# Attention scores of two heads of one half of the array per step, and products with v eight in a row

## Chip, cores and metric

One core of one Trainium2 chip. The metric is device time in microseconds (us) for one execution of the whole kernel; beside it stands one profiled execution whose trace is read here.

## What is computed

A transformer layer with attention and a feed-forward part side by side on the same normalised input: x is 2048 x 512, 32 heads of width 16, hidden width 1792.

```python
def _A_ref(x, wqkv, wo):
    qkv = (x @ wqkv).reshape(B, S, 3, H, Dh).transpose(2, 0, 3, 1, 4)
    q, k, v = qkv[0], qkv[1], qkv[2]
    scores = jnp.einsum("bhqd,bhkd->bhqk", q, k) * (Dh ** -0.5)
    p = softmax(scores, axis=-1)
    o = jnp.einsum("bhqk,bhkd->bhqd", p, v)
    return o.transpose(0, 2, 1, 3).reshape(B, S, D) @ wo

def _B_ref(x, w1, b1, w2, b2):
    return gelu(x @ w1 + b1) @ w2 + b2

xn = layernorm(A_x)
out = A_x + _A_ref(xn, A_wqkv, A_wo) + _B_ref(xn, B_w1, B_b1, B_w2, B_b2)
```

## The kernel before

The heads are worked in 8 groups of 4 (`NG`), the queries in 4 blocks of 512 (`NQB`); one head group and one query block is a `t`, and its 16 steps of 128 keys (or 128 queries for the maxima) are its units `u`, 512 units in all (`NU`). In each unit every one of the four heads gets two score products:

- **S** (`s_half`): scores with queries on the partitions, into a bank of the accumulator memory, of which VectorE takes the row maximum (`reduce_max` into `mt`, line 250). Three banks take turns.
- **T** (`e_half`): 20 units later (`LEAD`), when the maxima have gone through DRAM into the operand `qst`, the transposed scores with the maximum already subtracted; ScalarE writes exp of them into a tile `pe` (line 297). Three banks take turns.

**V** (`v_half`) multiplies the `pe` tiles in fp32 with v. Its sums stay in one bank for a whole `t`, the four heads in four quarters of 32 partitions. **D** is everything dense: the projections of q and k, the hidden layer (`hidden`, with a VectorE copy `hh` at line 978 and a chain on GpSimd), the product with `w2`, and at the end the output projection with `wo_s`. D comes in groups (`Group`), each summed in one bank and cut into 12 products (42 for `w2`) for each half of the array.

All four kinds are cut into products of 64 rows of operand and 32 output partitions (`tiled`), so the array works as two row halves, called side 0 and side 1, of four column quarters each. Heads 0 and 2 lie on side 0, heads 1 and 3 on side 1. V and D use both sides in turn, and both sides add into the same bank, so a side may begin only when the other has ended; a semaphore (`turns`, in `product`, `leave`, `enter`) orders that.

`unit` writes the order of the instructions by hand. A unit is two halves. Each half gives out the scores S side 0, T side 1, S side 1, T side 0, and then V for four heads on one side beside D on the other. The sides of V and D change in each half. D gives `pace` products to its side in each half: (4, 4) for `FAST`, (3, 4) for `MEAN`, (3, 3) for `SLOW`. A D group that ends hands its bank back at the end of the half.

`tick` runs once for each unit: it issues what was put off with `later` (transfers above all) and lets GpSimd have 2500 ns of queued work. All transfers go through the queue of SyncE.

Before the steady part stand about 140 us of normalisation, projection of the first heads and measuring of weights; behind it the last output projections.

Of the kernel before, what the change touches and what calls it, by code (L numbers as in the profile page):

```python
# [8 lines left out]
F32 = mybir.dt.float32  # L9
# [22 lines left out]
FAST, MEAN, SLOW = (4, 4), (3, 4), (3, 3)  # L32
MEASURE = (3, 0, 1, 2)
HALF = 1300
# [13 lines left out]
def layer_kernel(ctx: ExitStack, tc: tile.TileContext, x, wqkv, wo, w1, b1, w2, b2, out):  # L48
# [17 lines left out]
    w2_d = dram.tile([P, 2, NF, D], F16, name="w2_d")  # L66
    acc_d = dram.tile([S, D], F32, name="acc_d")
# [26 lines left out]
    wo_s = const.tile([P, 2, NC, D], F16, name="wo_s")  # L94
# [53 lines left out]
    def split_pool(hi, lo, src, inv):  # L148
        nc.scalar.activation(hi, src, AF.Copy, scale=inv)
        given("act", 1000)  # L150
        nc.gpsimd.tensor_scalar(src, src, inv, 0.0, op0=ALU.mult, op1=ALU.add)
        nc.gpsimd.tensor_tensor(lo, src, hi, op=ALU.subtract)
# [4 lines left out]
    backlog = {"act": 0, "dve": 0}  # L157

    def given(engine, ns):
        backlog[engine] += ns  # L160

    turns = tc.alloc_semaphore("turns")
    counted, left, newest, goal = [0], [], {}, [None]

    def product(user, *args, **kw):

        p = nc.tensor.matmul(*args, **kw)  # L169
        if user is None:  # L170
            return
        if goal[0] is not None:
            p._wait_ge(turns, counted[0])
            tc.declare_fence(p.ins, group=goal[0])
            goal[0] = None
        newest[user] = p

    def leave(user, goes_on):

        p = newest.pop(user, None)  # L180
        if p is not None and goes_on:
            p.then_inc(turns, 1)
            tc.no_tile_sem_insts.add(p.ins.name)
            counted[0] += 1
            left.append(p)

    def enter():

        if left:
            goal[0] = f"turn{counted[0]}"  # L190
            for p in left:
                tc.add_to_no_dep_group(goal[0], p.ins)
            left.clear()

    def tiled(user, dst, lhs, rhs, start, stop):

        for j in range(0, P, 32):
            product(user, dst[j:j + 32], lhs[:, j:j + 32], rhs, start=start, stop=stop)


    mt_of, ptiles, pv_of = {}, {}, {}
# [36 lines left out]
    def s_half(u, n):  # L238

        t, i = divmod(u, 16)  # L240
        g, qb = divmod(t, NQB)
        qt, kb = divmod(i, 4) if t else (i % 4, i // 4)
        if t not in mt_of:
            mt_of[t] = work.tile([P, 4, 4, 4], F32, name="mt", bufs=2)
        ks, qs = kst[g % 2], qst[g % 2]
        p, a = divmod(n, 2)
        r = slice(64 * a, 64 * a + 62)
        s = banks("S")
        tiled(None, s, qs[p][qb][r, qt * P:(qt + 1) * P], ks[p][kb][r, :], True, True)
        nc.vector.reduce_max(mt_of[t][:, n, qt, kb:kb + 1], s, axis=AX.X)  # L250
        given("dve", 600)

    def s_end(u):

        t, i = divmod(u, 16)
        if i < 15:
            return
        g, qb = divmod(t, NQB)
        qs = qst[g % 2]
        mneg = mnegs[t % 2]  # L260
        nc.vector.tensor_reduce(mneg[:, :16], mt_of[t].rearrange("p h t k -> p (h t) k"), axis=AX.X, op=ALU.max, negate=True)
        given("dve", 220)

        def store():

            pt = banks("S")
            for a in range(2):
                nc.tensor.matmul(pt[32 * a:32 * a + 32, :64], mneg[64 * a:64 * a + 64, :],
                                 ident[64 * a:64 * a + 64, 64 * a:64 * a + 64], start=True, stop=True)
            msb = work.tile([64, 64], F32, name="msb", bufs=2)  # L270
            nc.vector.tensor_scalar_mul(msb, pt[:64, :64], 1.0 / MROW)  # L271
            given("dve", 220)
# [12 lines left out]

    def e_half(u, n):
# [7 lines left out]
        tiled(None, st, kst[g % 2][p][kt // 4][r, k0:k0 + P], qst[g % 2][p][qb][r, :], True, True)  # L294
        pe = work.tile([P, QB], F32, name="pe", bufs=12)
        ptiles[u, n] = pe
        nc.scalar.activation(pe, st, AF.Exp, scale=sexp[:, g // 2:g // 2 + 1])  # L297
        given("act", 580)

    def v_half(u, a):  # L300

        t, kt = divmod(u, 16)
        g, qb = divmod(t, NQB)
        if kt == 0 and a == 0:
            pv_of[t] = hold("V", "S")
        pv = pv_of[t][0]
        r = slice(64 * a, 64 * a + 64)
        for h in (2, 3, 0, 1):
            c = (4 * g + h) * VW
            product("V", pv[32 * h:32 * h + 32, :], vv[r, kt, c:c + 32], ptiles[u, h][r],  # L310
                    start=(kt == 0 and a == 0), stop=(kt == 15 and a == 1))

    def v_end(u):

        t, kt = divmod(u, 16)
        g, qb = divmod(t, NQB)
        for h in range(4):
            del ptiles[u, h]
        if kt < 15:
            return  # L320
# [3 lines left out]
        given("act", 600)  # L324
# [12 lines left out]
        def inverse():  # L337
            nc.vector.reciprocal(dn, dn)
            given("dve", 330)
            later(1, lambda: nc.sync.dma_start(den_d[t, 1].rearrange("h (c q) -> (h c) q", q=32), dn))  # L340
# [63 lines left out]
    class Group:  # L404
# [15 lines left out]
        def product(self, side):  # L420
# [11 lines left out]
            tiled("D", self.bank, lhs[r], rhs[r], start, self.last and self.over())  # L432
# [43 lines left out]
    def project(m, w, sb, wh, bank, early=False):  # L476
# [6 lines left out]
        def finish(pj):  # L483
# [5 lines left out]
            given("act", 600)  # L489
# [62 lines left out]
    def ended():  # L552

        if cur[0] is not None and cur[0].over():
            done, cur[0] = cur[0], None
            done.end()
# [10 lines left out]
    def dense(gen, side):  # L567

        f = group(gen)
        for _ in range(0 if f is None else f.pace[pos[0] % 2]):  # L570
            if not f.usable(side):
                return
            f.product(side)

# [9 lines left out]
    def unit(gen):  # L584


        u = pos[0]
        e = u - LEAD
        if u == LEAD and cur[0] is not None:
            burst(gen, cur[0].left())  # L590
        pos[0] += 1
        for a in range(2):
            for b in range(2 * a, 2 * a + 2):
                if u < NU:
                    s_half(u, b)
                if 0 <= e < NU:
                    e_half(e, b ^ 1)
            if e >= 0:
                enter()

                w, r = (e - 2, 1) if a == 0 else (e - 1, 0)
                live = 0 <= w < NU
                new = r == 0 and w % 16 == 0
                if live and not new:
                    v_half(w, r)
                dense(gen, 1 - r)
                if live and new:
                    v_half(w, r)

                for user, goes_on in (("V", live and not (r == 1 and w % 16 == 15)),  # L610
                                      ("D", cur[0] is not None and not cur[0].over())):
                    leave(user, goes_on)
                for k in backlog:
                    backlog[k] = max(0, backlog[k] - HALF)
                if live and r == 1:
                    v_end(w)
                ended()
        if u < NU:
            s_end(u)
        if u < LEAD:  # L620
            burst(gen, LFILL[u - 16])
# [10 lines left out]
    with ExitStack() as st1:  # L632
# [16 lines left out]
        def absmax(dst, v):  # L649
            nc.vector.tensor_reduce(dst, v, axis=AX.XY if len(v.shape) == 3 else AX.X, op=ALU.max,  # L650
                                    apply_absolute_value=True)
            given("dve", 600)
# [229 lines left out]
        def prepare():  # L882
# [20 lines left out]
            for n in range(16):  # L903
# [5 lines left out]
                def then(wh=None, n=n):  # L909
# [8 lines left out]
                if n >= 14:  # L918
                    i = 2 * (n - 14)
                    split_steps(wo_s[:, 0, i:i + 2, :], wo_s[:, 1, i:i + 2, :], v, inv[:, 9:10], then)  # L920
                    continue
                wh = ph.tile([P, 2, 4, W] if n < 7 else [P, 2, 2, D], F16, name="wsp", bufs=2)
                k = n if n < 7 else 8
# [13 lines left out]
    def mlp():  # L937
# [5 lines left out]
        def gelu(hh, g, b, f):  # L943
            t1 = m2.tile([P, QB], F32, name="t1", bufs=2)

            def tanh():
                nc.scalar.activation(t1, t1, AF.Tanh, scale=GELU_C * GELU_A)
                given("act", 600)
# [14 lines left out]
        for b in range(NQB):  # L963
            xb = xbs[b]
            g = m2.tile([P, 2, NF, QB], F16, name="g", bufs=1)
            for f in range(NF):
# [8 lines left out]
                def hidden(hp, g=g, b=b, f=f):  # L975
# [3 lines left out]
                    given("dve", 700)  # L979
# [3 lines left out]
                             for c in range(NC) for i, j in PAIRS], dbank, hidden, pace=FAST if f % 2 else SLOW)  # L983
            for q in range(4):
# [7 lines left out]
                def store(yp, xa=xa, t=t):  # L992
                    yt = m2.tile([P, D], F32, name="yt", bufs=2)
                    nc.scalar.activation(yt, yp, AF.Copy, scale=gs[:, 2:3])  # L994
                    given("act", 600)
# [62 lines left out]
    with ExitStack() as st3:  # L1058
        p3 = pool(st3, "ph3")
        wo_l = p3.tile([64, 2, D], F16, name="wo_l")  # L1060
        nc.sync.dma_start(wo_l, wo_s[64:128, :, NC - 1, :])
# [67 lines left out]
```

## Time and profile before

| what | value |
|---|---|
| median of 3 runs | 1570.55 us (1565.78 to 1573.75) |
| the profiled execution | 1564.4 us, span 1562.6 us |
| granted TensorE clock | 0.992 of full speed |
| exps (line 297) / row maxima (line 250) | 2048 each, four of each in a unit |
| products of V / S / T, as instructions | 8192 each |

A step's time is read by counting exps in a stretch of the trace: four of them are one unit. TensorE, VectorE and ScalarE are each busy for most of the span, so a share of busy time says little; what counts in each stage is which of them the others wait for.

### The profile page before, as it was taken

How to read it: one execution, taken by the hardware profiler on the slowest of the kernel's cores; microseconds unless marked ns; L12 is line 12 of the kernel's file. 1: busy time of each engine (PE TensorE's matmuls, PEld its weight loads, DVE VectorE, ACT ScalarE, POOL GpSimd, SP SyncE). 2: the span in 40 equal slices, each digit the busy share in tenths (PEclk: the TensorE clock that was granted, in tenths of full speed). 3: DMA queues.
4: the chain of work that ended last, by engine and by line, in shares of the span. 5: the costliest groups of instructions: out<-in, count | busy, mean ns of one | idle time of the engine just before them, and what ended most of it. 6: DMA issues, size and time to landing. Idle time of an engine off the chain costs nothing.

```text
span 1562.6 us, 85974 instructions
## 1 busy us (share of the span) xinstructions
PE 1509.6 (97%) x38915; PEld 813.5 (52%) x38915; DVE 1419.0 (91%) x2388; ACT 1369.2 (88%) x2254; POOL 668.9 (43%) x742
## 2 busy tenths in 40 slices
PE   8997998989999999999999999999999999999998
PEld 4433554545555555555555555555555555554543
DVE  8886987989999999999999999999999999999911
ACT  4314997989999999999999999999999999999993
POOL 3113587737773111777411167751127773111000
PEclk9998999999999999999999999999999999999999
DMA  6467466351121111121111111221112100003123
GB/s 205 129 205 257 130 172 211 114 167 47 47 67 50 38 34 36 58 57 44 55 44 50 34 45 43 64 63 37 40 41 66 42 21 28 29 21 125 55 91 103
DMA packets 120248, 123.71 MB, mean 79 GB/s; under 512 B 38988, under 2 KB 90572, under 8 KB 119880
## 3 DMA queue, kind: packets, MB, share of 16 engines
q1 hardware_dynamic: 119880, 118.21, 25.0%
q8 instruction: 304, 4.98, 1.3%
q14 instruction: 64, 0.52, 0.1%
HBM read 80.61 MB, written 37.34 MB: 75 GB/s over the span
## 4 chain that ended last, share of the span: by engine, by line
PE 70%; DVE 21%; DMA 4%; issue 2%; POOL 1%; SPq 1%; ACT 1%; DVEq 0%; POOLq 0%
PE pV L169 21%; DVE mt L250 16%; PE pD L169 16%; PE pS L169 15%; PE pT L169 14%; DVE hh L978 2%; PE pD L428 1%; DMA wch<-in_B_w_dram 1%; PE pT L428 1%; DVE amx L650 1%; DMA dn<-den_d 1%; PE pT L521 1%; DMA m_d<-mhl 0%; PE pS L428 0%; DMA out_dram<-ac 0%
## 5 line engine op out<-in xcount | busy, mean ns | idle before, releaser
L297 ACT ACTIVATE pe<-pT,sexp 128x512 f32<-128x512 f32 x2048 | 1267.6, 688 | 72.8 <-PE pT L169 26.9
L250 DVE TENSOR_REDUCE mt<-pS 128x1 f32<-128x512 f32 x2048 | 1289.1, 683 | 34.4 <-PE pS L169 15.6
L169 PE MATMUL pV<-pe,vv 64*32 64x512 f32 x8192 | 1079.0, 597 | 1.4 <-PE pS L169 0.7
L169 PE MATMUL pT<-qst,kst 64*32 64x512 f16 x8192 | 706.9, 379 | 3.9 <-DMA qst<-m_d 1.4
L169 PE MATMUL pS<-kst,qst 62*32 62x512 f16 x8192 | 636.1, 379 | 35.6 <-DVE mt L250 32.1
L169 PEld LDWEIGHTS <-qst 62*32 62x32 f16 x8192 | 280.2, 92 | 273.5 <-issue 136.2
L169 PEld LDWEIGHTS <-kst 64*32 64x32 f16 x8192 | 294.1, 91 | 176.5 <-issue 68.6
L169 PE MATMUL pD<-w_s,g 64*32 64x512 f16 x5376 | 364.8, 377 | 0.0
L169 PE MATMUL pD<-xb,wc 64*32 64x512 f16 x5376 | 361.4, 378 | 0.0
L169 PEld LDWEIGHTS pV<-pe,vv 64*32 64x32 f32 x8192 | 181.6, 105 | 96.7 <-PE pS L169 7.6
L169 PEld LDWEIGHTS <-wc 64*32 64x32 f16 x5376 | 120.5, 92 | 52.6 <-issue 2.7
L169 PEld LDWEIGHTS <-g 64*32 64x32 f16 x5376 | 111.4, 91 | 44.4 <-issue 0.2
L169 PE MATMUL pD<-xt,wqk_h 64*32 64x512 f16 x1920 | 127.4, 382 | 0.7 <-issue 0.7
L996 POOL TENSOR_TENSOR xa<-xa,yt 128x512 f32<-128x512 f32 x16 | 20.4, 1276 | 238.8 <-ACT yt L994 238.8
L958 POOL TENSOR_TENSOR t<-hh 128x512 f32<-128x512 f32 x56 | 58.2, 1038 | 112.0 <-DVE hh L978 110.7
L348 POOL TENSOR_TENSOR osb<-osb,rb 128x512 f32<-128x512 f32 x31 | 39.9, 1286 | 150.5 <-DMA rb<-den_d 150.5
L274 POOL TENSOR_SCALAR mhl<-msb 64x64 f16<-64x64 f32 x32 | 7.6, 237 | 175.4 <-DVE msb L271 175.4
L960 POOL TENSOR_TENSOR t<-t,hh 128x512 f32<-128x512 f32 x56 | 71.7, 1280 | 4.7
L953 POOL TENSOR_TENSOR t<-t,hh 128x512 f32<-128x512 f32 x56 | 71.6, 1279 | 4.7
L955 POOL TENSOR_TENSOR g<-t,g 128x512 f16<-128x512 f32 x56 | 65.1, 1163 | 4.6
L169 PEld LDWEIGHTS <-wqk_h 64*32 64x32 f16 x1920 | 43.8, 93 | 16.1 <-issue 1.3
L169 PE MATMUL pD<-wo_s,oc 64*32 64x512 f16 x768 | 50.1, 378 | 0.0
(138 smaller groups left out, 869.5 us busy)
## 6 DMA issues: line engine op xcount, KB each, us to landing
wch<-in_B_w_dram SPq DMA_DIRECT2D x28, 512.0 KB
wc<-w_d SPq DMA_DIRECT2D x56, 256.0 KB
qk_d<-stg SPq DMA_DIRECT2D x32, 256.0 KB
rb<-den_d SPq DMA_DIRECT2D x124, 64.0 KB
kst<-qk_d SPq DMA_DIRECT2D x128, 48.0 KB
qst<-qk_d SPq DMA_DIRECT2D x128, 48.0 KB
xs<-in_A_x_dram SPq DMA_DIRECT2D x16, 256.0 KB
qk_d<-stg SPq DMA_DIRECT2D x32, 128.0 KB
```

The lines of the kernel that those rows point to most:

```text
L169: p = nc.tensor.matmul(*args, **kw)
L250: nc.vector.reduce_max(mt_of[t][:, n, qt, kb:kb + 1], s, axis=AX.X)
L297: nc.scalar.activation(pe, st, AF.Exp, scale=sexp[:, g // 2:g // 2 + 1])
L348: pooled((1280, lambda: nc.gpsimd.tensor_tensor(osb, osb, rb, op=ALU.mult)), (620, lambda: nc.gpsimd.tensor_scalar(ot[:, 0], osb, 1.0, 0.0 ...
L428: nc.tensor.matmul(self.bank, lhs, rhs, start=start, stop=self.last and self.over())
L521: nc.tensor.matmul(pj, xt[:, i, c, t * P:(t + 1) * P], wh[j][:, c, :], start=(n == 0), stop=(n == 11))
L953: (1280, lambda: nc.gpsimd.tensor_tensor(t1, t1, hh, op=ALU.mult)),
L955: (1160, lambda: nc.gpsimd.tensor_tensor(g[:, 1, f, :], t1, g[:, 0, f, :], op=ALU.subtract)),
L958: pooled((1040, lambda: nc.gpsimd.tensor_tensor(t1, hh, hh, op=ALU.mult)), (620, lambda: nc.gpsimd.tensor_scalar(t1, t1, 1.0, 1.0 / GELU_A ...
L960: (1280, lambda: nc.gpsimd.tensor_tensor(t1, t1, hh, op=ALU.mult)),
L978: nc.vector.tensor_scalar(hh, hp, scale, bias, op0=ALU.mult, op1=ALU.add)
L996: add = lambda: nc.gpsimd.tensor_tensor(xa, xa, yt, op=ALU.add)
```

## The change

`unit` is written anew. Units are taken in pairs. In a step with r = 0 the scores S and T of heads 0 and 2 (side 0) are made for both units of the pair, in the next step (r = 1) those of heads 1 and 3 (side 1). All V products of a step go to the other side, 1 - r: eight in two rounds of four, of what was exponentiated at least two steps before. D is given out in single portions: `pace` - 3 products on side r and then 3 on side 1 - r, where `pace` is now 8, 7 or 6 for `FAST`, `MEAN`, `SLOW`; every group of the hidden layer has `MEAN`. A D group that ends inside a step is followed at once by the next.

V and D have a semaphore each, and a product waits only where its own user changes sides. The `pe` tiles are 17 fixed ones (12 before); every eighth exp is given a dependence on an exp four before it. V's bank of a new `t` is taken from the S banks when the first V product of that `t` comes, and V of the old `t` is ended at the end of a step (`v_end`). To make room, `wo_s` no longer lies in SBUF throughout: its split halves are stored to DRAM (`wo_d`) and loaded at the start of the last stage. The counters `given` and `backlog`, which nothing read, are gone.

```diff
-FAST, MEAN, SLOW = (4, 4), (3, 4), (3, 3)
+FAST, MEAN, SLOW = 8, 7, 6
...
+        before = newest.get(user)
+        if before is not None and before[0] != side:
+            counted[user] += 1
+            before[1].then_inc(turns[user], 1)
...
+            p._wait_ge(turns[user], counted[user])
...
+    pes, used = [const.tile([P, QB], F32, name=f"pe{i}") for i in range(17)], [0]
...
+    def v_turn(a, step):
+        todo = {h: [w for w in due[a] if w[0] <= step and w[2] == h] for h in (a, 2 + a, 1 - a, 3 - a)}
+        due[a][:] = [w for w in due[a] if w[0] > step]
+        while any(todo.values()):
+            for h in todo:
+                if todo[h]:
+                    v_one(a, *todo[h].pop(0)[1:])
+            yield
+    def v_one(a, u, h):
+        t, kt = divmod(u, 16)
+        if t not in pv_of:
+            pv_of[t] = hold("V", "S")
...
-    def dense(gen, side):
-        f = group(gen)
-        for _ in range(0 if f is None else f.pace[pos[0] % 2]):
-            if not f.usable(side):
-                return
+    def dense(gen, side, n):
+        while n > 0 and (f := group(gen)) is not None and f.usable(side):
             f.product(side)
+            n -= 1
+            ended()
...
+        r = e % 2
+        v = v_turn(1 - r, pos[0] - (2 if e < NU else 0))
+        def score_s(i):
+            if u - r < NU:
+                s_half(u - r + i // 2, 2 * (i % 2) + r)
+        def score_t(i):
+            if e - r < NU:
+                e_half(e - r + i // 2, 2 * (i % 2) + r)
+        next(v, None)
+        dense(gen, r, (cur[0].pace if cur[0] is not None else FAST) - 5)
+        score_s(0)
+        score_t(0)
+        dense(gen, r, 1)
+        for _ in v:
+            pass
+        dense(gen, r, 1)
+        for i in (1, 2):
+            score_s(i)
+            score_t(i)
+        dense(gen, 1 - r, 1)
+        score_s(3)
+        dense(gen, 1 - r, 1)
+        score_t(3)
+        dense(gen, 1 - r, 1)
+        for t in [t for t in pv_of if summed[t] == [32] * 4]:
+            v_end(t)
...
-                             for c in range(NC) for i, j in PAIRS], dbank, hidden, pace=FAST if f % 2 else SLOW)
+                             for c in range(NC) for i, j in PAIRS], dbank, hidden, pace=MEAN)
...
+        wo_s = p3.tile([P, 2, NC, D], F16, name="wo_s")
         wo_l = p3.tile([64, 2, D], F16, name="wo_l")
-        nc.sync.dma_start(wo_l, wo_s[64:128, :, NC - 1, :])
+        nc.sync.dma_start(wo_s, wo_d)
+        nc.sync.dma_start(wo_l, wo_d[64:128, :, NC - 1, :])
```

More of the change, by code (lines that the diff above doesn't have):

```diff
@@ L431, in product @@
             self.at[side] += 1
-            tiled("D", self.bank, lhs[r], rhs[r], start, self.last and self.over())
+            tiled("D", side, self.bank, lhs[r], rhs[r], start, self.last and self.over())
         def over(self):
@@ L588, in unit @@
         e = u - LEAD
-        if u == LEAD and cur[0] is not None:
-            burst(gen, cur[0].left())
-        pos[0] += 1
[L592 to L617, printed above, removed]
@@ L618, in unit @@
-        if u < NU:
+        if e < 0:
+            pos[0] += 1
+            for n in range(4):
+                s_half(u, n)
+            s_end(u)
+            burst(gen, LFILL[u - 16])
+            tick()
+            return
+        if e == 0 and cur[0] is not None:
+            burst(gen, cur[0].left())
+        r = e % 2
[6 more added lines that the diff above has]
+                e_half(e - r + i // 2, 2 * (i % 2) + r)
@@ L619, in unit @@
+        for key in [k for k in ptiles if not any(w[1:] == k for side in due for w in side)]:
+            del ptiles[key]
+        pos[0] += 1
+        if u < NU and r:
             s_end(u)
-        if u < LEAD:
-            burst(gen, LFILL[u - 16])
         tick()
```

102 lines of the change are left out of this document (36 added, 66 removed).

## Prediction

> **What bounds the kernel now.** First the page: the span, the busy shares and the chain of waits.
>
> ```profile
> span 1562.6 us, 85974 instructions
> ...
> PE 1509.6 (97%) x38915; PEld 813.5 (52%) x38915; DVE 1419.0 (91%) x2388; ACT 1369.2 (88%) x2254; POOL 668.9 (43%) x742
> ...
> PE 70%; DVE 21%; DMA 4%; issue 2%; POOL 1%; SPq 1%; ACT 1%; DVEq 0%; POOLq 0%
> ```
>
> TensorE (PE) carries 70% of the chain, VectorE (DVE) 21%. Both are near full, so an average decides nothing, and I took the windows view for the exps of line 297 alone, cut where groups of the hidden layer and of the w2 product end. Columns: stretch, its length, busy time and count of exps; four exps are one step.
>
> ```profile
> core 0: us, ACT busy (x), PEclk, DMA share, GB/s
> 164.40:316.40 152.00, 126.90 (x205) 0.98 0.55 161
> ...
> 606.10:740.20 134.10, 121.84 (x197) 1.00 0.18 53
> 740.20:886.70 146.50, 137.69 (x224) 1.00 0.15 45
> 886.70:1022.40 135.70, 121.89 (x197) 1.00 0.18 51
> 1022.40:1150.70 128.30, 119.12 (x192) 1.00 0.15 44
> 1150.70:1285.60 134.90, 121.68 (x197) 1.00 0.17 47
> ...
> 1412.90:1441.30 28.40, 26.15 (x45) 1.00 0.51 160
> 1441.30:1488.00 46.70, 43.04 (x71) 1.00 0.23 71
> 1488.00:1535.00 47.00, 44.85 (x73) 1.00 0.32 97
> ```
>
> Projections (164 to 316) take 2.97 us a step. The hidden layer (606, 887, 1151) takes 134.9 us on average for 49.25 steps, 2.74 each. The w2 product takes 2.62 where its pace is SLOW (740, 56 steps) and 2.67 where it is MEAN (1022, 48 steps). Between the MLP and the output projection (1413) 11.25 steps without D take 2.52; output projection beside S (1441) 2.63; after the last S, T and V alone with D (1488), 2.58.
>
> What sets such a step is seen in the timeline of TensorE in the SLOW stage (start, length, count of products):
>
> ```profile
> 800.50 0.63 PE L169 MATMUL pV<-pe,vv 64*32 64x512 f32 x4
> 800.54 0.61 PE L169 MATMUL pD<-w_s,g 64*32 64x512 f16 x8
> 800.95 0.61 PE L169 MATMUL pV<-pe,vv 64*32 64x512 f32 x4
> 800.98 0.39 PE L169 MATMUL pD<-w_s,g 64*32 64x512 f16 x4
> 801.20 0.39 PE L169 MATMUL pS<-kst,qst 62*32 62x512 f16 x4
> 801.32 0.09 PEld L169 LDWEIGHTS <-kst 64*32 64x32 f16 x1 [0.23 <-issue]
> 801.38 0.59 PE L169 MATMUL pT<-qst,kst 64*32 64x512 f16 x8
> 801.42 0.26 PEld L169 LDWEIGHTS <-kst 64*32 64x32 f16 x3
> 801.60 0.40 PE L169 MATMUL pS<-kst,qst 62*32 62x512 f16 x4
> 801.79 0.62 PE L169 MATMUL pV<-pe,vv 64*32 64x512 f32 x4
> ```
>
> From one V to the next, a half, 1.29 us. Four products that run together fill one slot of one side; the half is six slots of 0.215 us: V four (two times two), then one of S and one of T. The side with D has only 3 + 2 = 5 slots of work, yet the half isn't shorter: its last T gets one weight load at 801.32 and the other three from 801.42 on, behind V on the other side. So a half is V + 2 whatever the pace is, 12 slots a step, 2.58 us.
>
> The other bound is VectorE. From the chain and its timeline:
>
> ```profile
> 795.29 2.40 DVE mt L250 x4
> ...
> 1169.41 0.81 DVE L978 TENSOR_SCALAR hh<-pD,fac,b_s 128x512 f32<-128x512 f32 x1
> 1124.32 0.33 DVE L338 RECIPROCAL dn<-dn 64x32 f32<-64x32 f32 x1
> 1415.11 7.64 ACT L297 ACTIVATE pe<-pT,sexp 128x512 f32<-128x512 f32 x13
> ```
>
> When it is late, four maxima take 2.40 us. In the hidden layer 14 hh copies come in 49 steps, 0.23 a step; the small operations that come once in 16 steps (0.33 and two of its kind or shorter) are 0.05. That is 2.68 for VectorE against 2.58 for TensorE: the hidden layer is VectorE's (2.74 measured, 2% above its bound), the w2 product is TensorE's (VectorE 2.45). ScalarE's exps take 0.588 each in a row, 2.35 a step, third.
>
> **The change part by part.** *The new order, pace 7.* Side r gets 4 D + 4 S + 4 T = 12 slots, the other 8 of V + 3 D = 11, with the D of the second side placed after V. The second V round starts in slot 4, as the first ends; D of side 1-r in slots 9 to 11, between T and S of side r. The step is 12 slots again, 2.58. So MEAN stages of w2 (96 steps, 2.67) gain only what evener spacing saves: I take 2.64, -3 us.
>
> *Pace 6.* Side r has 11 slots, the other 11: 2.37 us. Now VectorE's 2.45 binds, with ScalarE at 2.35 plus its copies and TensorE just below. Three engines so close wait for each other: the hidden layer shows 2% where two are 4% apart; I take 2.50, so 112 steps x (2.62 - 2.50) = -13 us. Ends: 2.45 (-19) and 2.58 (-4).
>
> *The hidden layer.* D per step falls: 12 products per side with 4 on one and 3 on the other; after three steps one side has done 11 and the other 10, and in the fourth step one side is empty for part of its portions, which is not made up because the next group may start only when both are done. Counting this through 14 groups gives 51.5 steps instead of 49. The MLP ends 10 steps later in all, in the stretch at 1413 where D now idles (2.52 a step), so this is no loss of steps. VectorE then needs 2.40 + 0.81 x 14/51.5 + 0.05 = 2.67. TensorE has 14 x 24 / 51.5 = 6.5 D, 11.5 slots, 2.47, and falls further behind that bound; I take 2.69. Before: 196 x 2.74 + 10 x 2.52 = 562; after: 206 x 2.69 = 554, -8 us. Ends: 2.67 (-12), 2.76 (+6).
>
> *Pace 8* (projections, output projection). Side r has 5 + 8 = 13 slots, 2.80, where it was 12. Projections take 2.97 with transfers, weight maxima and copies that hide most of this; I take 4 us for 60 steps, from 0 to 60 x 0.215 = 13. Output projection beside S: some 14 steps x (2.80 - 2.63) = +2.5 us.
>
> *After the last S.* Now 20 steps of 2.58. The timeline there:
>
> ```profile
> 1513.74 0.60 PE L169 MATMUL pD<-wo_s,oc 64*32 64x512 f16 x8
> 1514.14 0.41 PE L169 MATMUL pT<-qst,kst 64*32 64x512 f16 x8
> 1514.57 0.63 PE L169 MATMUL pV<-pe,vv 64*32 64x512 f32 x4
> 1515.88 0.63 PE L169 MATMUL pV<-pe,vv 64*32 64x512 f32 x4
> ```
>
> V waits for the semaphore of the last D: that ends at 1514.34 and V starts 0.23 us later, one T slot being too little to cover it. In the new order V changes sides with three or more slots between, and a step has 9 slots on side r, 11 on the other, 2.37 us: 20 x (2.58 - 2.42) = -3 us.
>
> *The new wait of D.* D changes sides inside a step. Its last product on side r starts in slot 5 (1.08 us), ends 0.38 later, and by the 0.23 us above the other side may start at 1.69; it is planned for slot 9, 1.94. Behind this wait in TensorE's queue stand S and T of the fourth pair, for which VectorE and ScalarE wait, so a miss costs the step its full length, but 0.25 us are in hand. V's new wait has three slots to spare. The dependence between exps is on one four back on the same engine, over long before: nothing.
>
> *S banks and V.* V of a new `t` now starts (heads 0 and 2) in the same step in which V of the old one ends (heads 1 and 3), and takes an S bank: for one step in 16 VectorE and TensorE share two banks instead of three. The fourth S then waits for the maximum of the second: written at 8 slots, read in 0.6 us, 11 slots, against a start in slot 10. Some 0.3 us in the half of the 32 cases in which TensorE paces, little in the others: +5 us. Ends: 0, and two reads each, 1.2 us x 32 = +38.
>
> *wo_s from DRAM.* 1 MB more in SyncE's queue at the start of the last stage, ahead of `wo_l`, the `oc` loads and the `dn` chain. What a transfer behind large ones can cost is seen earlier, and the queue of the last stage is:
>
> ```profile
> 249.77 5.34 DMA dn<-den_d
> ...
> 1417.06 0.66 SPq L1061 DMA_DIRECT2D wo_l<-wo_s  x1
> ...
> L169 PE MATMUL pD<-wo_s,oc x100: 372/376/387, 1441.4 to 1449.8; 64*32 64x512 f16 x100
> ```
>
> There `dn` took 5.34 us and VectorE stood behind it. Today the first product with `oc` comes 24 us after 1417; with the MLP ending 10 steps later it follows the load almost at once. +4 us, between 0 and 8. At the end V drops its lag and waits for the last two exps, 1.2 us: +1.
>
> *Sum:* -3 - 13 - 8 + 4 + 2.5 - 3 + 5 + 4 + 1 = -10.5 us against the profiled execution's 1564.4, so 1554. That execution lies 6 us below the median of the runs shown, 1570.55; on that footing 1560.
>
> **Rivals.** *More: VectorE at its bound throughout.* If 17 `pe` tiles and S spaced by 4, 2, 2 and 4 slots (before 1 and 5) keep VectorE fed, w2 SLOW takes 2.45, the hidden layer 2.67, MEAN 2.60, and the banks cost nothing: -19 - 12 - 6 + 4 + 2.5 - 3 + 4 + 1 = -28, 1542. For it: at 11 slots TensorE (2.37) no longer stands in VectorE's way (2.45). Against: three engines within 4%.
>
> *Slower: the two-bank step.* If VectorE is behind at that step, all four S wait a read longer. It decides once VectorE is more than one read (0.6 us) late when V takes the bank, which the hidden layer, VectorE's own, often brings. At 1.2 us x 32 it is +38 instead of +5: 1560 + 33 = 1593. Against: a late VectorE still has the other bank to read, so its own time isn't lost.
>
> *Nothing changes.* The scores' cost to VectorE is the same before and after; if the waits just move, the gain at pace 6 is eaten by pace 8: 1570.
>
> *Strict order.* A mechanism in which no product starts before all earlier ones have started would hold D, S and T behind V's second halves, two slots in each round, 16 slots a step: 512 x 0.86 = +440, 2010. The rows at 800.54 and 800.95 speak against it: eight D started before the second half of V, which stands ahead of them. The Trainium skill states such a rule in "TensorE: Matmul & The Clock Gate", Part 3, The mechanism: matmuls start and end in program order, without reordering; these rows do not bear it out for the two halves of an fp32 product.
>
> **How the numbers follow.** Forecast 0.40, more 0.22, slower 0.30, nothing 0.06, strict order 0.02. A measurement of this kernel can tell about 0.5%, 8 us, from no change. The forecast's own range, by its ends, is 1546 to 1574: of its 0.40 some 0.23 lie over 0.5% faster and 0.17 within. Faster: 0.23 + 0.22 = 0.45; same: 0.17 + 0.06 + 0.02 of the slower case = 0.25; slower: 0.30. For 8 in 10 the range goes from inside the better case to the two-bank case, 1538 to 1596.
>
> **What would show it.** Right: 224 exps in some 140 us in the SLOW stages; the hidden layer at 2.69 a step with VectorE without gaps; 8 V products in two rounds 0.86 apart; the MLP ending some 10 steps later. Wrong: a step of 13 slots at pace 7 (a late D or V), S idle before VectorE's maxima once in 16 steps for over 0.5 us, projections over 3.1, or a stop of more than 8 us where `wo_s` is loaded.

## The result: 4.6% slower, and the profile after

The changed kernel takes 1639.58 us (median of 4 runs, 1637.52 to 1643.12) against 1569.37 us for the kernel before on the same chip: a ratio of 1.0458 with a 95% interval of 1.0424 to 1.0492. The forecast was 1560 us, with a range of 1538 to 1596. The prediction was wrong in sign and by 80 us in size.

The page of the kernel after: span, busy shares, the chain of waits, and the group of the maxima (busy time, mean ns of one, idle time of VectorE just before them).

```profile
span 1639.4 us, 85757 instructions
...
PE 1579.4 (96%) x38915; PEld 922.6 (56%) x38915; DVE 1410.5 (86%) x2388; ACT 1374.2 (84%) x2254; POOL 668.8 (41%) x742
...
PE 78%; DVE 11%; DMA 4%; POOL 3%; issue 2%; ACT 2%; SPq 1%; DVEq 0%; POOLq 0%
...
L236 DVE TENSOR_REDUCE mt<-pS 128x1 f32<-128x512 f32 x2048 | 1284.0, 683 | 118.4 <-PE pT L161 56.4
```

The same group on the page of the kernel before:

```profile
L250 DVE TENSOR_REDUCE mt<-pS 128x1 f32<-128x512 f32 x2048 | 1289.1, 683 | 34.4 <-PE pS L169 15.6
```

The maxima cost what they did (683 ns), but VectorE is idle before them for 118.4 us instead of 34.4: 84.0 more, where the span has grown by 76.8. TensorE's share of the chain goes from 70% to 78%, VectorE's from 21% to 11%. TensorE hands scores over too late; the work itself has not grown.

Where it happens, in the windows view of the exps of line 283, cut at the same events as before:

```profile
core 0: us, ACT busy (x), PEclk, DMA share, GB/s
164.00:325.00 161.00, 128.94 (x205) 0.99 0.55 159
...
629.20:772.20 143.00, 123.57 (x198) 1.00 0.18 50
772.20:923.90 151.70, 137.74 (x224) 1.00 0.15 42
...
1066.90:1203.70 136.80, 118.23 (x192) 1.00 0.14 40
...
1346.20:1481.50 135.30, 118.25 (x192) 1.00 0.08 23
1481.50:1503.00 21.50, 16.26 (x28) 0.92 0.71 229
...
1563.50:1611.00 47.50, 46.18 (x77) 1.00 0.30 90
```

Four exps are a step: the hidden layer takes 2.89 us a step (629; forecast 2.69), the w2 product 2.71 at pace 6 (772; forecast 2.50) and 2.85 and 2.82 at pace 7 (1067 and 1346; forecast 2.64). Only the tail, T without S, came as forecast: 2.47 (1563; forecast 2.42, before 2.58). The granted clock is 0.99 to 1.00 in these stages; it is 0.92 in the 21.5 us at 1481, where `wo_s` is loaded and a step takes 3.07 us.

The next table takes the steps from the starts of their last T products, and adds the best version of the experiments, E9 (which stays slower than before):

| steps | before | after | E9 | after, us in all |
|---|---|---|---|---|
| 0 to 64, projections | 2.96 | 3.15 | 3.07 | +12 |
| hidden layer, 4 x 52, with its edges | 2.78 | 2.93 | 2.81 | +31 |
| w2 product at pace 6, 2 x 56 | 2.62 | 2.73 | 2.63 | +12 |
| w2 product at pace 7, 2 x 48 | 2.65 | 2.85 | 2.75 | +19 |
| output projection beside S, 12 | 2.64 | 2.89 | 2.73 | +3 |
| after the last S, 19 | 2.59 | 2.49 | 2.53 | -2 |

They sum to 75 of the 76.8 us. Behind the last T there are 2.7 more. The loss is spread over every stage in which S, T, V and D run together.

What such a step looks like, in the timeline of TensorE at pace 7 (start, length, count):

```profile
1129.07 0.40 PE L161 MATMUL pD<-w_s,g 64*32 64x512 f16 x4
...
1129.54 0.61 PE L161 MATMUL pV<-pe,vv 64*32 64x512 f32 x4
...
1130.39 0.61 PE L161 MATMUL pV<-pe,vv 64*32 64x512 f32 x3
...
1130.60 0.61 PE L161 MATMUL pV<-pe,vv 64*32 64x512 f32 x1
1130.61 0.59 PE L161 MATMUL pD<-w_s,g 64*32 64x512 f16 x5
...
1130.82 0.38 PE L161 MATMUL pD<-w_s,g 64*32 64x512 f16 x2
1131.02 0.40 PE L161 MATMUL pS<-kst,qst 62*32 62x512 f16 x4
1131.05 0.59 PE L161 MATMUL pV<-pe,vv 64*32 64x512 f32 x1
...
1131.76 0.40 PE L161 MATMUL pD<-w_s,g 64*32 64x512 f16 x4
```

and in that of VectorE over the same step:

```profile
1129.12 2.48 DVE L236 TENSOR_REDUCE mt<-pS 128x1 f32<-128x512 f32 x4 [0.31 <-PE pS L161]
1131.80 1.89 DVE L236 TENSOR_REDUCE mt<-pS 128x1 f32<-128x512 f32 x3 [0.20 <-PE pT L161]
```

Two things are late. First D of the second side, called D' from here: the last D of side r starts at 1130.82 and ends at 1131.20, and D' starts at 1131.76, 0.56 after that end, where 0.23 was expected. What it follows is something else: it starts 0.71 after the start of V's last second half (1131.05), which lasts 0.59. Over 34 steps between 1105 and 1200 us this distance is 0.704 us in the median, 0.704 and 0.708 at the 5th and 95th percentile, while the distance from the start of the last D of side r varies between 0.86 and 1.08. Yet D' waits on D's own semaphore, which no V product touches. The trace also keeps the moments at which semaphores change: V's does so at 1131.66, D's at 1131.72, though D had ended at 1131.20. In all of the 34 steps D's change comes 0.059 to 0.060 us behind V's, and 0.35 to 0.68 behind D's own end. Second, the scores: the S products of 1131.02 end at 1131.42, and VectorE, idle, starts at 1131.80, 0.16 after V's second half ends at 1131.64. The semaphore it waits on changes at 1131.78, next behind D's.

### The profile page after: what moved, and what is told of

It reads as the page before. It is cut to its first block, busy times and chain, and to the rows that moved or that the text cites. A ratio compares the mean times of both kernels' runs of the same rounds, so it can differ in the third digit from the quotient of the medians.

```text
span 1639.4 us, 85757 instructions
## 1 busy us (share of the span) xinstructions
PE 1579.4 (96%) x38915; PEld 922.6 (56%) x38915; DVE 1410.5 (86%) x2388; ACT 1374.2 (84%) x2254; POOL 668.8 (41%) x742
## 4 chain that ended last, share of the span: by engine, by line
PE 78%; DVE 11%; DMA 4%; POOL 3%; issue 2%; ACT 2%; SPq 1%; DVEq 0%; POOLq 0%
PE pV L161 27%; PE pD L161 16%; PE pT L161 15%; PE pS L161 15%; DVE mt L236 7%; DVE hh L977 2%; ACT pe L283 1%; PE pD L418 1%; DMA wch<-in_B_w_dram 1%; DMA dn<-den_d 1%; PE pT L418 1%; POOL wsp L881 1%; DVE amx L653 1%; PE pT L510 1%; POOL wch L879 0%
## 5 line engine op out<-in xcount | busy, mean ns | idle before, releaser
L236 DVE TENSOR_REDUCE mt<-pS 128x1 f32<-128x512 f32 x2048 | 1284.0, 683 | 118.4 <-PE pT L161 56.4
L161 PE MATMUL pV<-pe,vv 64*32 64x512 f32 x8192 | 1064.8, 593 | 0.3 <-issue 0.3
L161 PE MATMUL pS<-kst,qst 62*32 62x512 f16 x8192 | 827.2, 380 | 37.2 <-DVE mt L236 35.2
L161 PE MATMUL pT<-qst,kst 64*32 64x512 f16 x8192 | 832.2, 378 | 9.7 <-DVE hh L977 6.1
L161 PEld LDWEIGHTS <-qst 62*32 62x32 f16 x8192 | 266.3, 91 | 231.9 <-issue 125.1
L161 PE MATMUL pD<-w_s,g 64*32 64x512 f16 x5376 | 384.8, 377 | 0.8 <-ACT pe L283 0.6
L161 PE MATMUL pD<-xb,wc 64*32 64x512 f16 x5376 | 379.6, 379 | 0.2 <-ACT pe L283 0.2
L161 PEld LDWEIGHTS pV<-pe,vv 64*32 64x32 f32 x8192 | 316.1, 106 | 85.3 <-issue 6.3
L161 PEld LDWEIGHTS <-kst 64*32 64x32 f16 x8192 | 259.1, 93 | 127.1 <-issue 26.6
L161 PEld LDWEIGHTS <-g 64*32 64x32 f16 x5376 | 158.3, 91 | 81.6 <-issue 48.9
L161 PEld LDWEIGHTS <-wc 64*32 64x32 f16 x5376 | 144.3, 91 | 67.2 <-issue 35.5
```

## The theories

**A, in its first form:** TensorE reports its products as done in program order. The last D of side r stands behind V's second round; it runs early, on the other rows of the array, but its signal comes only when the V products ahead of it have ended. **A, in its wide form,** formed when the first experiments gave back too little: this holds for S and T too, so that VectorE and ScalarE get late whatever stands behind a V round. **B:** V's second round stands too many instructions behind the first in the queue, so that it comes late itself (the fourth head of it starts at 1130.60, 0.21 behind the other three), and distance counts, not order. **Bunching:** S and T of a step come too close together for VectorE and ScalarE, whoever reports them. **Banks** (theory C in the expectations): the S bank that V takes when it begins a new `t` holds S up.

The ends of products in a trace are modelled. So these runs can't tell whether a product behind V ends late or is only told late; what they show is when its semaphore changes and when the engine that waits for it goes on.

Each run stands against the kernel before on its own chip, where that has a median between 1563.7 and 1569.4 us. What one run gains on another is therefore taken from the ratios, whose intervals are some 0.2 to 0.7% to either side.

## The experiments

**E1: the signalling D ahead of V's second round.** Both last D of side r come before it.

```diff
-        dense(gen, r, 1)
+        dense(gen, r, 2)
         for _ in v:
             pass
-        dense(gen, r, 1)
```

> Edit to the changed kernel: the last portion of D on side r is handed over ahead of the second round of V instead of behind it. Theory A (TensorE reports its products as done in program order, so the signal of that D portion, which stands behind V's second round, comes only when V's second halves are done; the D of the other side, and S and T behind it in the queue, wait for it): the signal now comes before V's second round, D on the other side starts behind the third T, and a step at pace 7 falls from a median of 2.78 us to about 2.62, in the hidden layer from 2.81 to 2.68, at pace 6 from 2.59 to 2.50; total about 1590. Theory B (V's second round is late because it stands more than 64 instructions behind the first): the round stands 8 instructions further back, steps get no shorter or up to 0.1 us longer, total 1640 to 1680. Theory C (the loss is the step with two S banks): no change, 1640.

Measured: 1626.81 us, 1.0389 (1.0353 to 1.0426), by the ratios 11 us below the changed kernel, where some 50 were expected. The median step at pace 7 falls from 2.78 to 2.62, in the hidden layer from 2.81 to 2.63, and D' no longer keeps 0.704 from V: D's semaphore now changes 0.03 us after D's end in the median (0.01 to 0.08). At pace 6 the median rises, 2.59 to 2.65, where a fall to 2.50 was expected. And the means fall less than the medians (hidden layer 2.93 to 2.88, counted as in the table): VectorE still waits. Its group of maxima:

```profile
L236 DVE TENSOR_REDUCE mt<-pS 128x1 f32<-128x512 f32 x2048 | 1279.2, 681 | 108.4 <-PE pS L161 47.5 <-PE pT L161 47.5 <-PE pD L161 0.2
```

108.4 us idle after 118.4. D's wait is real, and it is the smaller part.

**E4: both D behind V's second round,** the other way round.

```diff
-        dense(gen, r, 1)
         for _ in v:
             pass
-        dense(gen, r, 1)
+        dense(gen, r, 2)
```

> Edit to the changed kernel: both late portions of D on side r are handed over behind the second round of V, which so stands 8 instructions nearer to the first. Theory A alone (signals in program order): the D of the other side still waits for V's second halves; no change, 1640. Theory B alone (distance between the V rounds): the last head of V's second round starts 0.2 us earlier at pace 7 and the steps there fall from 2.78 to about 2.6, also in the hidden layer; at pace 6 no change; total about 1595. Both together (D waits for V's second halves and those are late by the distance): the same 1595, but D on the other side still starts 0.70 us behind the start of V's last second half, as now. Theory C (two S banks): no change.

Measured: 1638.94 us, 1.0467 (1.0439 to 1.0494): no change. V's second round is handed over eight instructions nearer to the first, and D' still starts 0.74 to 0.79 after V's last second half begins. The edit didn't bring the late head forward everywhere: at pace 7 in the w2 product it still starts 0.19 behind the first of its round, in the second hidden layer 0.06 instead of 0.19, and there too the step stays at 2.89. In E1 it was the other way: three heads of that round come 0.2 late instead of one, and the median step is shorter. So distance moves single heads, and order sets the step: B falls.

**E5: the whole order by A's first form,** D of side r and V first, all S and T behind them.

```diff
         next(v, None)
-        dense(gen, r, (cur[0].pace if cur[0] is not None else FAST) - 5)
-        score_s(0)
-        score_t(0)
-        dense(gen, r, 1)
+        dense(gen, r, (cur[0].pace if cur[0] is not None else FAST) - 3)
         for _ in v:
             pass
-        dense(gen, r, 1)
+        score_s(0)
+        score_t(0)
```

> Edit to the changed kernel: all of D on side r comes directly behind V's first round, then V's second round, then all S and T of the step. This removes both what theory A and what theory B name: the signal of D stands ahead of V's second round, and that round stands 48 instructions behind the first at pace 7. Theory A or B or both: pace 7 at about 2.60 us a step, hidden layer about 2.70, pace 6 about 2.50; with the step of two S banks still there (0.87 us once in 16 steps), total 1575 to 1590. Rival: with all S close together (spaced by 2, 2, 2 and 6 slots) VectorE runs dry once in a step: hidden layer above 2.8, total above 1620.

Measured: 1861.69 us, 1.1882 (1.1857 to 1.1908), a median step of 3.21: the largest miss of the study. A's first form had D' free and nothing else late. The timeline of E5:

```profile
1302.56 0.66 PE L161 MATMUL pV<-pe,vv 64*32 64x512 f32 x2
...
1302.82 0.40 PE L161 MATMUL pS<-kst,qst 62*32 62x512 f16 x3
...
1303.06 0.59 PE L161 MATMUL pV<-pe,vv 64*32 64x512 f32 x1
...
1303.79 1.89 DVE L236 TENSOR_REDUCE mt<-pS 128x1 f32<-128x512 f32 x3 [0.90 <-PE pS L161]
```

The first S ends at 1303.22. VectorE has been idle for 0.90 us and starts at 1303.79, 0.14 after V's last second half ends (1303.65). So S is held back just as D was. By its size bunching would explain E5 as well, and E8 tells them apart.

**E8: E5 with the first pair of S and T moved ahead of V's second round,** and nothing else: D, V and three of the four pairs stay as close together as in E5.

```diff
         dense(gen, r, (cur[0].pace if cur[0] is not None else FAST) - 3)
+        score_s(0)
+        score_t(0)
         for _ in v:
             pass
-        score_s(0)
-        score_t(0)
```

> Edit to the kernel with D first (V, all D of side r, V again, then all S and T; 1862 us): only the first S and T of the step move, from behind V's second round to ahead of it. Theory A, wide form (what stands behind a V round is reported when that round's second halves are done): VectorE, which stood idle there until 0.58 us after the end of the first S, starts within 0.1 us of it; the fourth S, which waits for the maximum of the first, comes earlier, and the step falls from 3.21 to 2.8 to 2.9 us, total 1660 to 1700. Rival (bunching: four S close together, spaced by 2, 2, 2 and 6 slots, leave VectorE dry): spacing is as good as unchanged, step 3.1 to 3.2, total above 1800.

Measured: 1630.82 us, 1.0401 (1.0331 to 1.047): 231 us from one moved pair, and a median step of 2.66. The timeline of E8:

```profile
1300.97 0.63 PE L161 MATMUL pV<-pe,vv 64*32 64x512 f32 x2
1301.01 0.38 PE L161 MATMUL pS<-kst,qst 62*32 62x512 f16 x2
...
1301.43 0.61 PE L161 MATMUL pV<-pe,vv 64*32 64x512 f32 x2
...
1301.45 2.60 DVE L236 TENSOR_REDUCE mt<-pS 128x1 f32<-128x512 f32 x4
```

The same S beside the same V, but handed over ahead of it: VectorE starts 0.06 us after S ends (1301.39), with V's second halves only just begun (1301.43). The second S, which stands behind that round, is again taken up 0.53 after its end in the median. Bunching, which needed over 1800 us, falls; A in its wide form stands. The gain was larger than expected; that a first S in time also frees its bank in time is the likely reason, not a shown one.

**E6: S and T of side r spread ahead of V's two rounds,** the order S0 T0, V, D, S1 T1, V, D D, S2 T2, then D' as before.

```diff
-        next(v, None)
-        dense(gen, r, (cur[0].pace if cur[0] is not None else FAST) - 5)
         score_s(0)
         score_t(0)
-        dense(gen, r, 1)
+        next(v, None)
+        dense(gen, r, (cur[0].pace if cur[0] is not None else FAST) - 5)
+        score_s(1)
+        score_t(1)
         for _ in v:
             pass
-        dense(gen, r, 1)
-        for i in (1, 2):
-            score_s(i)
-            score_t(i)
+        dense(gen, r, 2)
+        score_s(2)
+        score_t(2)
```

> Edit to the changed kernel: in each step the first S and T stand ahead of V's first round and the second S and T ahead of V's second round (before: behind them); the rest as in the changed kernel, both late D portions of side r behind V. Theory A in its wide form (TensorE reports in program order, so every S and T handed over behind a V round is reported only when that round's second halves are done, and VectorE and ScalarE stand idle meanwhile, as VectorE does before the first S of each step in the kernel with D first: 0.58 us from the end of S to its start against 0.08 in the kernel before): the first three S are now reported at once, VectorE's idle time in the hidden layer falls from about 0.25 us a step to under 0.1; hidden layer 2.91 to about 2.75, MEAN 2.86 to 2.70, pace 6 2.73 to 2.60; total about 1585. D on the other side still waits for V's second halves, about 0.4 slots past its place. Rival B' (TensorE itself is short of slots, the late reports don't matter): steps as in the changed kernel or as with the last D portion ahead of V, total 1625 to 1640. Rival C (two S banks make most of the loss): the step in 16 with two banks stays 0.8 us longer than the others, and the total stays above 1610.

Measured: 1605.91 us, 1.0256 (1.0233 to 1.0279), by the ratios 32 us below the changed kernel and less than the 55 expected, with the group of maxima at

```profile
L236 DVE TENSOR_REDUCE mt<-pS 128x1 f32<-128x512 f32 x2048 | 1287.7, 682 | 77.6 <-PE pS L161 45.3 <-PE pT L161 16.5
```

77.6 us idle, 41 less. Where VectorE had been idle it now starts 0.05 us after S ends in the median; in the changed kernel it was 0.43 for the second S.

**E9: E6 and E1 together.**

```diff
         score_s(1)
         score_t(1)
+        dense(gen, r, 2)
         for _ in v:
             pass
-        dense(gen, r, 2)
```

> Edit to the kernel with the first two S and T ahead of V's rounds (1606 us): the late D portions of side r move ahead of V's second round too. If what is left there is D's wait for V's second halves (0.76 us behind their start, some 0.5 slots past its place): pace 7 falls from a median of 2.77 to 2.66, total 1585 to 1595. Against it works that V's second round stands 16 instructions further behind the first (64 at pace 7 instead of 48): if that distance counts, V's second round comes 0.2 to 0.3 us later and the gain is gone, 1600 to 1620.

Measured: 1592.67 us, 1.0157 (1.0109 to 1.0205). The two parts add up within the noise: by the ratios 11 for D and 32 for S and T, and 47 for both, of the 70 us that the change cost. It is the best order found, and still slower than the kernel before.

**E10: E6 with projections and output projection at pace 7 instead of 8.**

```diff
-FAST, MEAN, SLOW = 8, 7, 6
+FAST, MEAN, SLOW = 7, 7, 6
```

> Edit to the kernel with the first two S and T ahead of V's rounds (1606 us): the pace of projections and output projection is 7 instead of 8. If the projections' 13 slots cost them (3.08 us a step over the first 64 steps against 2.96 in the kernel before): their step falls to about 2.95, and as they then last some 9 steps more, which the idle steps behind the MLP take up, the total falls by 3 to 8 us, 1598 to 1603. If transfers and VectorE hide the 13th slot: no change, 1606.

Measured: 1614.38 us, 1.0296 (1.0249 to 1.0342). Steps 0 to 64 fall from 3.08 to 2.93 as expected: the 13 slots of pace 8 do cost the projections about 0.15 us a step. But the time doesn't fall: the intervals of the two runs overlap, and the profiled one is 8.6 us longer. Up to the last T it is 4 us ahead of E6's; the loss lies behind. The MLP ends at step 487 instead of 464, where 9 steps had been reckoned with, so the loads of `wo_s` and `oc` come while the last S are given out. In one step of 13.41 us TensorE waits 8.1 for `oc`, and VectorE stands,

```profile
1514.24 0.69 DVE L236 TENSOR_REDUCE mt<-pS 128x1 f32<-128x512 f32 x1 [9.00 <-PE pS L161]
```

and behind the last T 43.9 us pass instead of 30.9. Pace 8 costs time where it stands; by these two profiles it saves that again behind.

**E7: the changed kernel, V's bank of a new `t` from the T banks.**

```diff
-            pv_of[t] = hold("V", "S")
+            pv_of[t] = hold("V", "T")
...
-        free_banks["S"].append(k)
+        free_banks["S" if t == NG * NQB - 1 else "T"].append(k)
```

> Edit to the changed kernel: V's bank of a new t is lent by the T banks instead of the S banks (the last one goes back to S). Theory C: the step in which V of the old and of the new t overlap (the third of 16) lost 0.87 us because VectorE and TensorE shared two S banks; it now loses that on T's side, where ScalarE's 0.59 us a piece leaves a little more room: 0.4 to 0.8 us over the other steps, with ScalarE instead of VectorE as the one waited for; total 1625 to 1640. If the loss came from something else in that step (the order of V's eight products over two banks), it stays 0.87 and VectorE stays the one waited for. Theory A has no part in it: all other steps as in the changed kernel.

Measured: 1638.95 us, 1.0477 (1.0451 to 1.0502), as without the edit. In the changed kernel the step in which V begins a new `t` takes 3.58 us, its neighbours about 2.70, an excess of 0.87; here it takes 3.52. The waits of the changed kernel (us in total, times, longest):

```profile
PE pS L161 <- DVE mt L236: 35.2, 58, 8.4
...
PE pT L161 <- ACT pe L283: 1.6, 7, 0.2
```

and those of E7:

```profile
PE pS L161 <- DVE mt L236: 23.8, 28, 8.3
...
PE pT L161 <- ACT pe L283: 6.4, 31, 0.2
```

The wait moved from S to T, and the step stayed long. So moving the missing bank doesn't help; whether a bank too few on either side costs this much, E7 can't tell. In E6, with two S banks in that step as in the changed kernel, it takes 2.94 and the one behind it 2.89, where their neighbours take about 2.70: some 0.4 together. About half of the excess went with the order.

**E11: E9 with the edit of E7,** to see whether the banks are what keeps E9 above before.

> The order with S, T and D of side r ahead of V's second round is still 25 us (1.0157) above before. Its steps are 0.11 and 0.35 us longer than before's in the second and third of every 16, where V of a new t takes an S bank: 32 x 0.46 = 15 us. This kernel takes V's bank from the T banks and gives it back to them. If the two S banks make these steps long now that the late reports are mostly gone: they fall to 2.65 to 2.77 and the time to about 1577. If it is the V rounds themselves, which write two banks there: steps and time stay, 1589 to 1596, and T waits for ScalarE's exps somewhat more than before.

Measured: 1597.41 us, 1.0211 (1.0166 to 1.0255), not faster than E9. The second and third step of every 16 stay at 2.94 and 2.99 (E9 2.88 and 3.00, before 2.77 and 2.65). Here too it doesn't help to move the missing bank; a run in which neither S nor T lacks one is not among these.

**E12 and E13: do V products in two banks split a round?** In E9's step with a new `t` V's rounds run two and two instead of four at a time. The timeline of E9 over such a step and the next:

```profile
778.74 0.60 PE L161 MATMUL pV<-pe,vv 64*32 64x512 f32 x2
778.94 0.62 PE L161 MATMUL pV<-pe,vv 64*32 64x512 f32 x2
779.17 0.60 PE L161 MATMUL pV<-pe,vv 64*32 64x512 f32 x2
779.39 0.60 PE L161 MATMUL pV<-pe,vv 64*32 64x512 f32 x2
779.60 0.60 PE L161 MATMUL pV<-pe,vv 64*32 64x512 f32 x2
...
781.04 0.40 PE L161 MATMUL pS<-kst,qst 62*32 62x512 f16 x4 [0.20 <-DVE mt L236]
781.08 0.63 PE L161 MATMUL pV<-pe,vv 64*32 64x512 f32 x4
```

There heads 1 and 3 still add to the old bank while 0 and 2 begin the new one. E12 lets V of a `t` use two banks always (heads 0 and 2, heads 1 and 3; one is taken from T); E13 keeps one, with the T bank left unused. Both take the sums out at the end of a `t` with four copies in place of one. What E12 has over E13:

```diff
-    free_banks = {"S": [0, 1, 2], "T": [3, 4], "D": [6], "V": [7]}
+    free_banks = {"S": [0, 1, 2], "T": [3, 4], "D": [6], "V": [7, 5]}
...
-            pv_of[t, 0] = hold("V", "S")
+            pv_of[t, h % 2] = hold("V", "S")
```

> The order with S, T and D of side r ahead of V's second round, but V of a t lies in two banks throughout: heads 0 and 2 in one, heads 1 and 3 in a second one that T gives up; at the end of a t four copies of 32 partitions take the sums out instead of one. So each round of four V products writes two banks, as it did so far in one step of 16 only, where the round was seen to run two and two and V's first start to last start took 2.80 us instead of 2.15. If the two banks in one round are what splits it: V takes about 2.8 in every step, and the step grows by some 0.4 to 0.65, 200 to 330 us over the run with one V bank and two T banks. If the split has another cause (the change of t, the first product of a sum): both runs agree within 10 us.

> The same with V of a t in one bank, and a T bank left unused, four copies at the end of a t: it is what the other is compared with. Two T banks instead of three let T wait for ScalarE's exp and four copies take 32 x 1.5 us more of ScalarE, which has 100 us idle: 1595 to 1640 by either theory, V from first to last start 2.15 us, 2.8 in one step of 16.

Measured: E12 1822.46 us, 1.1643 (1.1577 to 1.171); E13 1828.57, 1.1682 (1.1627 to 1.1737). They agree within the 10 us that stood for no effect, the median step is 3.03 in both, V's first start to last start 2.65 in both, and E12's rounds run four at a time, or three and one, as E13's do:

```profile
902.38 0.64 PE L161 MATMUL pV<-pe,vv 64*32 64x512 f32 x4
...
903.26 0.60 PE L161 MATMUL pV<-pe,vv 64*32 64x512 f32 x3
903.46 0.61 PE L161 MATMUL pV<-pe,vv 64*32 64x512 f32 x1
```

Two banks do not split a round. E13's own forecast missed: two T banks instead of three, with the three more copies, cost 236 us over E9, not 3 to 47. The median step is 0.38 us longer, some 195 us in 512 steps; the third step of every 16 takes 5.25 instead of 3.00 us, and what part the copies have in that was not told apart. By theory A a T that is held back keeps its bank longer; that this is why is argued here, not shown.

## Why the prediction was wrong, step by step

**The new wait of D: the step that failed.** It took the end of D's last product on side r plus 0.23, with 0.25 us in hand. But D's semaphore changes right behind V's, and D' starts 0.704 us after V's last second half does, whenever D itself has ended. In the changed kernel that closes a loop from step to step: from D' (1129.07) over S and T of the fourth pair to V of the next step (1129.54) 0.47, V's two rounds to the last second half (1131.05) 1.51, then 0.71 to D' (1131.76). That is 2.69 us for 2.58. Undone, it gives 11 us (E1), or some 15 on top of E6 (E9).

**S and T: the larger part, and a term that wasn't in the sum.** The plan of slots counted when S runs, not when VectorE is told. Where VectorE is idle, it takes up an S behind a V round 0.43 us after its end in the median (0.53 in E8, 0.67 in E5), one ahead of it after 0.05. The prediction said that VectorE would bind at pace 6 with 2.45 us a step and that evener S would feed it better; they run more evenly and arrive less so. E6 gives back 32 us. D and S together are 47 of the 70 us.

**Hidden layer and MLP end.** 51.5 steps were forecast, and the MLP ending 10 steps later. It took 198 exps, 49.5 steps: when a group ends together with a step, the next step has no current group and runs at pace 8. The MLP ended at step 464, before at 465, and not 10 steps later. So the 8 us of gain forecast there had a wrong count under it as well as a wrong step (2.89 for 2.69).

**Pace 8** in the projections: 0 to 13 us for 60 steps were given and 4 taken. Steps 0 to 64 cost 12 us in the changed kernel and 7 in E9, and E10 shows that the slots are the cause: right in kind, taken too small.

**S banks:** 5 us were taken. The step in question lost 0.87 x 32 = 28 us. About half of that went when the scores were told in time, with the banks as they were (E6). Whether the other half is the missing bank stays open: E7 and E11 only move it from S to T.

**`wo_s` from DRAM and the end of V:** 4 and 1 us were taken. The issue of the load and the wait for `dn` that follows, in the timelines of SyncE and VectorE after,

```profile
1485.68 0.35 SPq L1059 DMA_DIRECT2D wo_s<-wo_d  x1
...
1497.94 0.34 DVE L329 RECIPROCAL dn<-dn 64x32 f32<-64x32 f32 x1 [2.23 <-DMA dn<-den_d]
```

and the same wait before:

```profile
1422.15 0.35 DVE L338 RECIPROCAL dn<-dn 64x32 f32<-64x32 f32 x1 [1.45 <-DMA dn<-den_d]
```

0.8 us more. The step with that wait and the next take 5.30 and 3.42 us; before they took 4.13 and 2.38. That is 2.2 us, near what was taken. **The tail** (V changing sides with slots between) came as forecast, 2.47 for 2.42. D changes sides there too, and D' still starts 0.704 us behind V's last second half in the median of ten times; why that costs the step nothing there is not shown.

**The rivals.** The slower one gave 1593 by another mechanism, the two-bank step, and would have been wrong by 47 us. Strict order was set aside because D started before V's second half. That still holds: in the rows above S at 1131.02 starts before V at 1131.05. What was missed is the other half of the rule. The Trainium skill, "TensorE: Matmul & The Clock Gate", Part 3, The mechanism, says that matmuls start and also end in program order, so that a semaphore on the last of them is sound. For starts the rows contradict it, for the moment at which a product is told they agree: D's semaphore changes 0.06 us behind V's, and D' goes on 0.704 us behind V's last start. The prediction refuted the rule by its starts and dropped its ends with them.

**What stays open.** E9 is 25 us above before. By the table 7 are the projections, 10 the w2 product at pace 7 and 6 the hidden layer. Seen another way, in the steps from 96 to 460, the second and third step of every 16, where V passes to a new `t`, are 0.11 and 0.35 longer than before, 32 x 0.46 = 15 us. V's rounds are split two and two there, and V takes 2.80 us from first to last start instead of 2.15. It does not go when T lends the bank instead of S (E11), and two banks in one round are not what splits it (E12). The row at 781.04 has an S waiting 0.20 us for a maximum just there, so a bank too few remains a rival. An order in which heads 0 to 3 change `t` in the same round was not tried.

## What to carry to other kernels

In a plan of time slots, give every product two times: when it runs, and when its waiter is told. In these runs the second was no earlier than the end of the fp32 products handed to TensorE ahead of it, though they ran on other rows. So hand over what another engine (or the other side) waits for ahead of long fp32 products, not behind them; and when a rule has a start and an end, test both before it is set aside.

## What the runs showed that was not expected

Products on different rows of the array overlap and pass each other in starting, but not in being told: D handed over behind a V round was told 0.06 us after V in all of 34 steps, up to 0.68 us after its own end. S behind such a round was taken up 0.43 to 0.67 us after its end, ahead of it 0.05. Moving one pair of S and T past that round is worth 231 us in 512 steps, 0.45 a step (E5 to E8). Taking one of three T banks away, with three more copies at the end of each `t`, cost 236 us in E9's order (E13), and 0.38 us of the median step.
